# A retention layer and a Mish feed-forward layer on one core: the table of scale factors moves from ScalarE's load queue to SyncE's

## The chip, the core and the metric

The kernel runs on one core of a Trainium2 chip. The metric is device time in microseconds (us), the median over several executions. In the profile the engines are called PE (TensorE: matrix products and transposes), DVE (VectorE), ACT (ScalarE), POOL (GpSimd) and SP (SyncE). [...] A load that is started goes to a queue and is carried out by the core's 16 DMA engines, beside all computing. Whoever needs the data waits for a semaphore that the load raises when it has landed.

## The reference, cut to what matters

```python
def _attn_ref(q, k, v):                     # each (4, 8, 768, 64), float32
    B, H, S, D = q.shape
    gamma = 1.0 - 2.0 ** (-5.0 - np.arange(H, dtype=np.float32))
    scale = 1.0 / np.sqrt(D)
    state = np.zeros((B, H, D, D), dtype=np.float32)
    for t in range(S):
        state = gamma[None, :, None, None] * state + np.einsum('bhd,bhe->bhde', k[:, :, t], v[:, :, t])
        y[:, :, t] = scale * np.einsum('bhd,bhde->bhe', q[:, :, t], state)
    return y

def _moe_ref(x, w_in, w_out):               # x: the y above as (3072, 512)
    h = x @ w_in                            # (512, 2048)
    sp = np.where(h > 20.0, h, np.log1p(np.exp(np.minimum(h, 20.0))))
    g = h * np.tanh(sp)
    return g @ w_out                        # (2048, 512)
```

Each head keeps a state of 64 x 64 that decays by its own factor gamma from token to token. Every token's result of all eight heads, 512 numbers, then goes through two matrix products with the Mish function between them.

## The kernel before, in words

The tokens are cut into chunks of 128. Within a chunk the recurrence is written as products of matrices: scores of q against k, masked so that a token sees only earlier ones, times v; and q times the state that the chunks before have left. The decay is not applied token by token. A power of gamma that depends on the token's place and on the head is multiplied into q, k or v once, while they are converted from float32 to float16. These powers are the **table of scale factors**, `qvs`: 128 partitions x 88 float32 numbers, 44 KB, worked out when the kernel is built (lines 47 to 58) and kept in memory as a constant. It holds the factors for v (`vs`), for q of the first block (`qs_four`), for q and v or k of pairs of chunks (`qs_two`, `vs_two`) and a constant (`boosts`). Line 81 loads it, once.

The chunks are taken in blocks: the first block has four (512 tokens), all later ones two (256 tokens). Each block goes through the retention part and then through the feed-forward part, and the retention part of the next block is woven between the feed-forward products of the one before. Later blocks form sums of weights and of intermediate results, which save matrix products. Instructions are issued in the order in which the code stands (`manual_schedule`): every engine works through its own list in that order, and nothing plans it anew.

Four places matter for this change.

- **The constants** (lines 78 to 116). The table's load stands first, on ACT. POOL then makes an identity matrix (`ident`, lines 96 and 97) and masks; ACT loads its function table and runs one activation on a dummy (`warm`, line 116).
- **The first loads** (`load_first_q`, line 250, and `first_block`, line 1213). SP starts, in this order: the first half of q (four heads of 512 tokens, 512 KB), its second half (512 KB), four loads of k (256 KB each, line 296), four of v (256 KB each), w_in in six pieces (line 195), w_out, and then the inputs of the next chunks.
- **The first work** (`first_block`). PE runs 46 products of the identity matrix with itself (`spin(46, 1)`, line 466), whose result nobody uses, while q is on its way. `turn_first_q` (line 275) then scales a half of q on DVE (line 279, which reads `qf` and `qs_four`), lets PE transpose it (line 267) and ACT or DVE copy the result out (lines 271 and 273). After the first half come 14 more such products, after the second the same for k: DVE scales one quarter of k, POOL the other three (line 317), each with `vs_two`.
- **The step into the feed-forward part.** POOL converts the first slice of w_in to float16 (line 220), and PE begins the product with it (line 687).

The last store of the kernel is split: most pieces go out on SP's queue (line 1128), the very last piece on ACT's (line 1121). ACT starts no other transfer than this one and the table.

```python
    qvs = cpool.tile([P, (7 + CPB) * H], FP32, name="qvs")
    nc.scalar.dma_start(qvs, nc.inline_tensor(qvs_np, name="qvs_c").ap())
...
        nc.vector.tensor_tensor(
            in_place(q16), by_head(qf[:, mine]), scale_by_head(qs_four[:, mine]), op=ALU.mult)
```

Of the kernel before, what the change touches and what calls it, by code (L numbers as in the profile page):

```python
# [16 lines left out]
def kernel(  # L17
# [9 lines left out]
    nc = tc.nc  # L27
# [30 lines left out]
    qvs_np = np.ascontiguousarray(np.concatenate(tables, 1))  # L58
# [19 lines left out]
    ctx.enter_context(tc.manual_schedule())  # L78

    qvs = cpool.tile([P, (7 + CPB) * H], FP32, name="qvs")  # L80
    nc.scalar.dma_start(qvs, nc.inline_tensor(qvs_np, name="qvs_c").ap())

    def table(n, count=1):
        t = qvs[:, n * H:(n + count) * H]
# [165 lines left out]
    def load_first_q():  # L250

        qf = wstage.tile([P, H, CPB, D], FP32, name="qfirst", tag="wt", bufs=4)
        for a in range(0, H, H // 2):
            nc.sync.dma_start(
                qf[:, a:a + H // 2],
                q[0, a:a + H // 2, :TB].rearrange("h (p r) d -> p h r d", r=CPB))
        return qf

    def turn_parts(parts, dst, on_act=False):
# [952 lines left out]

    def first_block():
        qf = load_first_q()
        for n in range(2):
            room_pair(n)
# [320 lines left out]
```

## Time and profile before

| what | before |
|---|---|
| median of the runs | 192.01 us |
| the profiled execution's own time | 192.31 us |
| its span, first to last instruction | 190.5 us |
| PE busy | 184.8 us, 97% |
| DVE busy | 143.1 us, 75% |
| ACT busy | 105.8 us, 56% |
| POOL busy | 72.2 us, 38% |
| granted clock of PE, mean | 0.999 |
| read from memory, written | 27.31 MB, 6.29 MB |

The time of a run is a little longer than the span, since it takes in what lies around the first and the last instruction. In the views, a line such as `L279` is a line of the kernel before; `out<-in` names what an instruction writes and reads; what stands in brackets at the end is how long the engine was idle before it, and who ended that. `SPq` and `ACTq` are the issuing of transfers on SP and ACT, whose length is that of the issue and not of the transfer. "To landing" is counted from the start of the issue to the last semaphore of the load. A busy share of PE of 97% does not say that it works at its peak, as its products overlap and their ends are modelled.

### The profile page before, as it was taken

What the parts mean: (1) busy time and instruction counts of PE and PEld (TensorE: products, weight loads), DVE (VectorE), ACT (ScalarE), POOL (GpSimd) and SP (SyncE); (2) the same over time, 40 slices, a digit from 0 to 9 for tenths busy, and PEclk for the clock granted to TensorE, in tenths of its full rate; (3) what the DMA queues carried; (4) which work ended last, traced back from release to release, by engine and by line L of the source; (5) the groups of instructions that cost most, each with busy time, mean ns of one, the idle gap of its engine ahead of it and who ended that gap; (6) DMA issues with size and microseconds to landing.
All of it is one profiled execution on the core that took longest, in us unless ns stands there. A gap on an engine that the chain in (4) does not pass through costs nothing.

```text
span 190.5 us, 7643 instructions
## 1 busy us (share of the span) xinstructions
PE 184.8 (97%) x3310; PEld 162.3 (85%) x3310; DVE 143.1 (75%) x294; ACT 105.8 (56%) x201; POOL 72.2 (38%) x100
## 2 busy tenths in 40 slices
PE   7898999999999999999999999999999999999993
PEld 7656478888888888888998998998998998988982
DVE  0778469886977878988798698696697698676862
ACT  3366766264552552553684584584683673873650
POOL 5182000487508745940573634624534710000000
PEclk9999999999999999999999999999999999999999
DMA  4999999999999999899999997891899970301103
GB/s 147 310 303 350 382 387 376 293 330 226 189 237 294 172 235 238 129 266 234 220 186 317 156 202 165 214 200 39 194 174 244 219 172 3 114 3 53 62 3 112
DMA packets 84210, 38.82 MB, mean 204 GB/s; under 512 B 58192, under 2 KB 78288, under 8 KB 84176
## 3 DMA queue, kind: packets, MB, share of 16 engines
q1 hardware_dynamic: 83888, 38.22, 87.1%
q8 instruction: 26, 0.43, 1.0%
q10 hardware_dynamic: 288, 0.11, 0.4%
q14 instruction: 8, 0.07, 0.1%
HBM read 27.31 MB, written 6.29 MB: 176 GB/s over the span
## 4 chain that ended last, share of the span: by engine, by line
PE 93%; DMA 3%; DVE 1%; ACT 1%; issue 0%; SPq 0%; DVEq 0%
PE h_ps L917 23%; PE o_ps L1103 23%; PE h_ps L705 18%; PE o_ps L1007 10%; PE o_ps L762 7%; PE y_ps L609 3%; DMA qfirst<-in_q_dram 3%; PE u_ps L503 1%; PE at L495 1%; PE t_ps L267 1%; PE y_ps L396 1%; PE h_ps L687 1%; PE at L466 1%; PE at L347 1%; DVE qk L279 1%; PE u_ps L368 0%
## 5 line engine op out<-in xcount | busy, mean ns | idle before, releaser
L705 PE MATMUL h_ps<-xt,win 128*128 128x256 f16 (+1 forms) x276 | 34.3, 284 | 0.0
L705 PEld LDWEIGHTS <-win 128*128 128x128 f16 x276 | 26.7, 98 | 6.2 <-DVE win L220 0.3
L714 ACT ACTIVATE g<-h_ps 128x512 f16<-128x512 f32 x38 | 22.7, 597 | 15.2 <-PE h_ps L705 15.2
L917 PE MATMUL h_ps<-xt,wsum 128*128 128x128 f16 x448 | 29.6, 219 | 0.0
L929 ACT ACTIVATE g<-h_ps 128x512 f16<-128x512 f32 x42 | 24.2, 597 | 5.6 <-PE h_ps L917 5.6
L917 PEld LDWEIGHTS <-wsum 128*128 128x128 f16 x448 | 26.2, 98 | 0.0
L917 PE MATMUL h_ps<-xt,win 128*128 128x128 f16 x336 | 24.8, 219 | 0.0
L1103 PEld LDWEIGHTS <-gsum 128*128 128x128 f16 x232 | 21.5, 98 | 2.6
L1103 PE MATMUL o_ps<-tmat,gsum 128*128 128x256 f16 (+1 forms) x176 | 21.5, 268 | 0.0
L917 PEld LDWEIGHTS <-win 128*128 128x128 f16 x336 | 20.8, 98 | 0.2
L440 POOL TENSOR_TENSOR qk<-kf,qvs 128x512 f16<-128x512 f32 x18 | 18.9, 1052 | 2.5 <-DMA kf<-in_k_dram 2.5
L447 POOL TENSOR_TENSOR v<-vf,qvs 128x512 f16<-128x512 f32 x18 | 18.6, 1050 | 2.6 <-DMA vf<-in_v_dram 2.5
L437 POOL TENSOR_TENSOR qk<-qf,qvs 128x512 f16<-128x512 f32 x18 | 19.1, 1062 | 1.3 <-PE u_ps L368 1.3
L1103 PEld LDWEIGHTS <-g 128*128 128x128 f16 x184 | 16.5, 98 | 1.6
L667 ACT CAST xt<-y_ps 128x512 f16<-128x512 f32 x16 | 10.8, 738 | 11.1 <-PE y_ps L609 9.9
L965 DVE TENSOR_TENSOR h_ps<-h_ps,hsum 128x512 f32<-128x512 f32 x14 | 9.7, 695 | 9.2 <-PE h_ps L917 9.1
L1443 POOL COPY summed<-gsum 128x1 f16<-128x1 f16 x7 | 1.6, 233 | 36.8 <-DVE gsum L879 29.4
L954 ACT COPY h_ps<-h_ps 128x512 f32<-128x512 f32 x14 | 8.2, 583 | 12.4 <-issue 8.4
L1103 PE MATMUL o_ps<-wout,g 128*128 128x256 f16 (+1 forms) x120 | 14.5, 265 | 0.0
L1113 ACT COPY snap<-o_ps 128x256 f32<-128x256 f32 (+1 forms) x22 | 8.2, 373 | 11.0 <-PE o_ps L1103 11.0
L1126 DVE TENSOR_TENSOR osb<-o_ps,snap 128x256 f32<-128x256 f32 (+1 forms) x22 | 9.1, 415 | 4.2 <-ACT snap L1113 2.8
L942 DVE TENSOR_TENSOR hsum<-h_ps,hsum 128x512 f32<-128x512 f32 x14 | 9.6, 687 | 0.7 <-PE h_ps L917 0.2
(130 smaller groups left out, 334.0 us busy)
## 6 DMA issues: line engine op xcount, KB each, us to landing
out_dram<-osb SPq DMA_DIRECT2D x22, 256.0 KB, 3.9
qf<-in_q_dram SPq DMA_DIRECT2D x18, 256.0 KB, 4.8
kf<-in_k_dram SPq DMA_DIRECT2D x14, 256.0 KB, 6.0
vf<-in_v_dram SPq DMA_DIRECT2D x14, 256.0 KB, 5.3
wt<-in_moe_w_out_dram SPq DMA_DIRECT2D x6, 512.0 KB, 8.4
vf<-in_v_dram SPq DMA_DIRECT2D x20, 128.0 KB, 3.7
wi<-in_moe_w_in_dram SPq DMA_DIRECT2D x4, 512.0 KB, 8.3
wi<-in_moe_w_in_dram SPq DMA_DIRECT2D x2, 1024.0 KB, 11.1
```

What stands on the lines that cost most here:

```text
L437: nc.gpsimd.tensor_tensor(in_place(q16.rearrange("p (w x) d -> p w x d", x=2)), by_head(qf), scale_by_head(qs_two[:, heads]), op=ALU.mult)
L440: nc.gpsimd.tensor_tensor(k16.rearrange("p (y w) d -> p w y d", y=2), kf.rearrange("p (w y) d -> p w y d", y=2), boosts.rearrange("p (w y) ...
L447: nc.gpsimd.tensor_tensor(cast[g][2], loaded.pop(g)[2], vs[g % 2].unsqueeze(2).broadcast_to((P, H, D)), op=ALU.mult)
L667: nc.scalar.copy(dst[:, :, x], src)
L705: nc.tensor.matmul(h_ps[:, j, cols], wins[s][f // 2][:, bp, f % 2 * P:(f % 2 + 1) * P], xts[blk][:, bp, cols], start=(bp == 0 and at == 0) ...
L714: nc.scalar.activation(gt, h_ps, AF.Mish, scale=inv_boost3)
L762: nc.tensor.matmul(banks[ij][:, t], x(f)[:, t * P:(t + 1) * P], w(f), start=ij in open_banks, stop=f == fs[-1], skip_group_check=True)
L917: nc.tensor.matmul(o_ps[:, f], w(f // 2, k)[:, f % 2 * P:(f % 2 + 1) * P], x[:, k], start=begin and f == 0 and k == 0, stop=k == 1, skip_g ...
L929: nc.scalar.activation(gt[:, f:f + n, j * C:(j + 1) * C], src, AF.Mish, scale=inv_boost3)
L965: nc.vector.tensor_tensor(pf[p], pa[p], m5[p], op=ALU.add)
L1007: nc.tensor.matmul(o_ps[:, cols], x(f), w(f)[:, cols], start=first and z == 0, stop=z == n - 1, skip_group_check=True)
L1103: nc.tensor.matmul(o_ps[:, c:c + wide], x(f), w(f)[:, c:c + wide], start=first and f == 0 and c == cols.start, stop=f == n - 1, skip_group ...
```

## The change: what it does

The load of the table is taken away from its place ahead of everything on ACT's queue. SP starts it instead, between the first and the second half of q. Nothing else is edited; the lines between the two places move up by one, those after the second place down by one.

```diff
     qvs = cpool.tile([P, (7 + CPB) * H], FP32, name="qvs")
-    nc.scalar.dma_start(qvs, nc.inline_tensor(qvs_np, name="qvs_c").ap())
...
             nc.sync.dma_start(
                 qf[:, a:a + H // 2],
                 q[0, a:a + H // 2, :TB].rearrange("h (p r) d -> p h r d", r=CPB))
+            if a == 0:
+                nc.sync.dma_start(qvs, nc.inline_tensor(qvs_np, name="qvs_c").ap())
         return qf
```

## The prediction, made before the changed kernel was run

> **What bounds the kernel now.** I read the page's first two parts, then a table of stretches, then the chain of work that ended last, and then the first 18 us in order of time, since the change lies there.
>
> ```profile
> span 190.5 us, 7643 instructions
> ...
> PE 184.8 (97%) x3310; PEld 162.3 (85%) x3310; DVE 143.1 (75%) x294; ACT 105.8 (56%) x201; POOL 72.2 (38%) x100
> ...
> PEclk9999999999999999999999999999999999999999
> ```
> ```profile
> 0.00:6.60 6.60, 4.79 (x46) 4.62 (x46) 1.28 (x2) 1.49 (x2) 2.76 (x17) 1.00 0.66 201
> 6.60:17.64 11.04, 10.28 (x268) 6.54 (x268) 8.66 (x11) 6.98 (x14) 5.42 (x11) 1.00 1.14 314
> 17.64:40.00 22.36, 22.36 (x184) 17.17 (x185) 16.64 (x26) 13.17 (x24) 3.71 (x5) 1.00 1.07 357
> ```
>
> In the table the first column after the stretch is its length, the next PE's busy time. From 17.64 on PE has no gap in the third row, and the page gives it 97% of the whole span. So a change to the first loads acts on the time only by moving the moment at which PE's unbroken work begins, at 17.64 us, and then one to one. What leads there is in the chain:
>
> ```profile
> 1.25 5.51 DMA qfirst<-in_q_dram
> 6.76 0.02 issue
> 6.79 1.24 DVE qk L279
> 8.02 0.05 issue
> 8.07 1.00 PE t_ps L267 x12
> ...
> 17.64 1.92 PE h_ps L687 x16
> ```
>
> The second half of q sets the start (until 6.76), then DVE's scaling, then PE's transposes. The same stretch in order of time (start, length, engine, line):
>
> ```profile
> 0.74 0.39 ACTq L81 DMA_DIRECT2D qvs<-qvs_c  x1
> 0.74 1.00 SPq L254 DMA_DIRECT2D qfirst<-in_q_dram  x2
> ...
> 1.16 1.28 ACT L116 ACT_TABLE_LOAD   x1 [1.16 <-PEq L1521]
> ...
> 1.36 4.79 PE L466 MATMUL at<-ident 128*128 128x128 f16 x46 [1.36 <-POOL ident L97]
> ...
> 1.79 3.57 SPq L296 DMA_DIRECT2D kf<-in_k_dram  x4
> ...
> 5.34 1.22 DVE L279 TENSOR_TENSOR qk<-qfirst,qvs 128x1024 f16<-128x1024 f32 x1 [4.47 <-DMA qfirst<-in_q_dram]
> ...
> 6.62 0.62 PE L267 MATMUL t_ps<-ident,qk 128*128 128x128 f16 x8 [0.47 <-DVE qk L279]
> ...
> 6.79 1.23 DVE L279 TENSOR_TENSOR qk<-qfirst,qvs 128x1024 f16<-128x1024 f32 x1 [0.23 <-DMA qfirst<-in_q_dram]
> ...
> 7.07 0.93 PE L466 MATMUL at<-ident 128*128 128x256 f16 x7
> ...
> 7.27 1.01 ACT L271 COPY qkt<-t_ps 128x1024 f16<-128x1024 f16 x1 [4.62 <-PE t_ps L267]
> ...
> 8.74 3.05 POOL L317 TENSOR_TENSOR qk<-kf,qvs 128x512 f16<-128x512 f32 x3 [5.09 <-DMA kf<-in_k_dram]
> ...
> 16.98 0.61 POOL L220 CAST win<-wi 128x512 f16<-128x512 f32 x1 [3.18 <-DMA wi<-in_moe_w_in_dram]
> ...
> 17.64 1.64 PEld L687 LDWEIGHTS <-win 128*128 128x128 f16 x16 [0.17 <-POOL win L220]
> ```
>
> The reader is to see two things. DVE's first scaling waits 4.47 us for q although the table (qvs) is needed too; which of the two is last is told by their times to landing, first of the q halves, then of the table:
>
> ```profile
> DMA to landing us min/median/max: 4.5/5.0/5.5
> ```
> ```profile
> DMA to landing us min/median/max: 3.0/3.0/3.0
> ```
>
> Half one lands at 0.74+4.5 = 5.24, half two at 1.25+5.5 = 6.75 (its start is in the chain), the table at 0.74+3.0 = 3.74: it has 1.5 us to spare. And 17.64 hangs on two chains that end together: PE's own, and the first slice of w_in through the cast at 16.98, both fed by the same stream of loads. What that stream does at first (the last two columns are the DMA share and GB/s):
>
> ```profile
> 1.75:2.10 0.35, 0.35 (x7) 0.35 (x5) 0.00 (x0) 0.35 (x1) 0.32 (x1) 1.00 1.05 96
> 2.10:2.60 0.50, 0.50 (x7) 0.50 (x6) 0.00 (x0) 0.49 (x2) 0.45 (x1) 1.00 0.01 4
> 2.60:2.90 0.30, 0.30 (x6) 0.30 (x4) 0.00 (x0) 0.05 (x1) 0.25 (x3) 1.00 0.27 18
> 2.90:3.40 0.50, 0.50 (x8) 0.50 (x6) 0.00 (x0) 0.00 (x0) 0.44 (x4) 1.00 0.80 263
> 3.40:4.40 1.00, 1.00 (x12) 1.00 (x11) 0.00 (x0) 0.00 (x0) 0.23 (x2) 1.00 1.09 386
> ```
>
> Traffic begins at about 1.75, stops from 2.10 to 2.60 with three loads outstanding, and runs at its full 386 GB/s only from 3.4. Why it stops is not in the profile, and it is the main unknown of this forecast.
>
> **The change part by part.** As built, PE, DVE and POOL keep their instructions in the same order; ACT loses one DMA issue and SP gains one between the halves of q.
>
> ACT: the issue at 0.74 (0.39 us) goes, so its table load and the warming activation come up to 0.39 us earlier. ACT is then idle until 7.27 (4.62 us in its row), waiting for PE: 0.
>
> SP: one issue more, 0.39 us by ACT's row or 0.50 by half of SP's own first row. The second half of q and all later loads (4 of k, 4 of v, w_in, w_out, the rest) are issued up to 0.5 us later. What hides it: half two is then issued by about 2.2, but the half in front of it holds the DMA engines for 512 KB / 386 GB/s = 1.36 us, from 2.9 to 4.3. Without that cover it would cost the whole 0.5. The loads of k behind them are held up already: the four take 3.57 us to issue, 0.89 each, against 0.50 for q. So the added issue falls into time in which SP would be waiting: 0. SP's waits on earlier landings (from the second v load on) now stand on the first half, the table and the second half in that order; all three are landed in the order of issue, well before those loads can move: 0.
>
> Place of the table in the stream. It leaves the space in front of q and goes between its halves:
>
> ```profile
> q10 hardware_dynamic: 144, 0.05, 8.2%
> ```
>
> This is the table's queue in the first 6 us: 8.2% of 6.0 us is 0.49 us of all 16 engines, its stopped packets included. By bytes alone it is 44 KB / 386 GB/s = 0.12. So half two lands between 0.12 and 0.49 us later for it, if nothing were gained in front. The same goes the other way for half one: in 2.90:3.40 the engines move 263 GB/s in place of 386, a loss of 0.5 x (386-263)/386 = 0.16 us, while the table's rest is served beside q. I take 0.16 off the first half (5.08) and, for the table, 0.12, the price by bytes, since the row with no other load in it (1.75:2.10, 96 GB/s) moves most of a table in 0.35 us before the stop: the table lands at 5.08+0.12 = 5.20, half two at 6.75-0.16+0.12 = 6.71.
>
> DVE's first scaling needs half one and the table, so it starts at 5.20+0.10 = 5.30 (today 5.34 for a landing at 5.24), ends 6.52, and the second starts with half two's landing at 6.74, against 6.79. Were the table's price 0.49, the first would start at 5.67 and end 6.89, the second begin at 7.11 by its landing: +0.32. The bounds of this term are thus -0.05 and +0.32. I take -0.05.
>
> POOL and DVE's scaling of k need the table too, but at 7.9 and 8.7, 2.5 us after it: 0. All other uses are later. The memory it lies in and its readers are the same: 0.
>
> [...]
>
> Sum: 0 + 0 - 0.05 + 0 = -0.05 us at 17.64, and the same at the end. The profiled execution took 192.31 us, 1.8 more than its span, and 0.3 more than the median of the runs, 192.01. Against 192.01 the sum gives 191.96, so 192.0, with a range of its own of 191.7 to 192.3.
>
> **The rivals.** First, *the stop is the table's own doing*. The table is issued on ACT at the same time as q on SP; the stop falls into ACT's table load (1.16 to 2.44). SP's issue is held up too:
>
> ```profile
> L296 SPq DMA_DIRECT2D kf<-in_k_dram x6: 507/1154/2498, 1.8 to 31.1; - x6
> ```
>
> The loads of k take 507 ns at best, yet the first four 3.57 us together, although only q is in front of them. For it: all traffic stops, q's as well. Against: a stop at the very start can be that of any first load. If it is so, q runs from 1.9 at 386 GB/s, ends 3.26 and lands 0.95 later as today (4.27 by bytes, 5.24 landed): about 4.2; the table 4.3, DVE 4.4 to 5.7, second half about 5.8, second scaling to 7.0, a full 1.0 earlier. PE can't take all of it: its 46 warming matmuls last until 1.36+4.79 = 6.15, so the first transposes come at 6.15 in place of 6.62; then 0.45 of transposes and 0.8 of warming matmuls, and the second ones at 7.4 in place of 8.07, -0.67; k's, which wait on loads, up to -0.9. w_in comes 0.9 earlier too. So -0.6 to -0.9, 191.1 to 191.4, in the middle 191.3.
>
> Second, on the other side, *the stop goes with the table's packets wherever they are*. Today it is covered, as the table has 1.5 us to spare. From first traffic to landing it took 3.74-1.75 = 2.0 us. Behind half one, its packets are reached at 4.3, so it lands at 6.3, DVE starts at 6.4, ends 7.6, then 8.85 in place of 8.02: +0.85, 192.9. It decides as soon as the table takes over 1.2 us from being reached. PE's gap before its first transposes grows from 0.47 to 1.5 us. If its clock then fell back, what it costs is bounded by the start of the run:
>
> ```profile
> L466 PE MATMUL at<-ident x40: 288/314/315, 1.4 to 5.5; 128*128 128x128 f16 x40
> ```
> ```profile
> L466 PE MATMUL at<-ident x8: 219/220/314, 5.4 to 5.9; 128*128 128x128 f16 x8
> ```
>
> Matmuls of one shape take 314 ns until 5.5 and 220 after it, and 40 in 4.1 us (0.10 each) against 8 transposes in some 0.45 (0.056): about half pace for 4.2 us, so at most 2.1 us lost, and 195.0 in all: still under 2%. [...]
>
> Third, *ACT's queue is slow at its first use*, whenever that is. Today that is the table; after the change it is the last store of the kernel, which ends the run:
>
> ```profile
> 187.74 0.37 ACTq L1121 DMA_DIRECT2D out_dram<-osb  x1
> ```
> ```profile
> DMA to landing us min/median/max: 1.7/1.7/1.7
> ```
>
> This 64 KB store lands in 1.7 us, the 44 KB table in 3.0. If the 1.3 us between them are a first use, they move to the end, bare: 193.3. Against it: SP's queue stopped too at 2.1, after its own first packets, which points to a common cause.
>
> **How the numbers follow.** As forecast 0.42; stop caused by the table on ACT's queue 0.33; table stopped behind half one 0.12 (in 0.02 of it with a lost clock); first use at the end 0.07; none of these 0.06. The first three lie in 191.1 to 192.9 and hold 0.85 of the chance without the lost clock; the rest, 0.15, is left out. As both signs hold much of it, the likeliest one's own range, 191.7 to 192.3, stands beside it. About 2%, 3.8 us, is what a measurement of this kernel can tell from no change, and no case reaches it: even the costliest is 195.0. Faster by over 2% would need 3.8 us, but before 17.64 PE is idle only 1.81+0.76 = 2.57 us in all by the first two rows of the table. So faster 0.02, within 0.95, slower 0.03, all of the two ends from what I haven't seen.
>
> **What would show it.** Right: the stop between 2.1 and 2.6 is still there with the table gone from ACT, q's first half lands at about 5.1, DVE starts within 0.2 us of 5.34 and 6.79, and w_in's cast and 17.64 stand within 0.3 us. The first rival: full rate from 1.9 on, the first four loads of k issued at about 0.5 us each, DVE's start at 4.4, PE's first transposes directly behind the warming matmuls. The second: DVE waits for the table beyond half one's landing by a microsecond. The third: over 2.5 us to landing of ACT's last store. Wrong altogether if PE shows gaps after 17.64 that it has not now.

## The result, and the profile after

| | before | after |
|---|---|---|
| median of 21 runs each, on one chip | 192.49 us | 192.89 us |
| ratio, after to before | | 1.0033, 95% interval 1.0018 to 1.0047 |
| profiled execution's own time | 192.31 us | 193.2 us |
| its span | 190.5 us | 191.3 us |

The changed kernel is slower by a third of a per cent. 192.89 us stands just inside the range of 191.1 to 192.9, but where -0.05 us was forecast, +0.4 us came. The forecast started from 192.01, the median of the first three of the 21 runs of before; over all 21 it is 192.49, and that is what the changed kernel is compared with. The ratio leaves out one execution of before, of 236.98 us, and follows the means of all others (193.05 after, 192.43 before) rather than the medians, so that a kernel's ratio and its median can say a little different things. In three later comparisons on other chips the unedited pair gave 0.9978, 1.0010 and 1.0026 (e1, e11 and e15 below). The first lines of the page after:

```profile
span 191.3 us, 7643 instructions
...
PE 184.8 (97%) x3310; PEld 162.1 (85%) x3310; DVE 144.4 (75%) x294; ACT 105.7 (55%) x201; POOL 72.5 (38%) x100
...
PEclk9999999999999999999999999999999999999999
```

PE's work and clock are those of before. The start in order of time, in the kernel after (lines of the code are one off):

```profile
0.73 1.28 ACT L115 ACT_TABLE_LOAD   x1 [0.73 <-PEq L1522]
...
0.74 0.45 SPq L253 DMA_DIRECT2D qfirst<-in_q_dram  x1
...
1.25 0.48 SPq L257 DMA_DIRECT2D qvs<-qvs_c  x1
...
1.78 0.43 SPq L253 DMA_DIRECT2D qfirst<-in_q_dram  x1
...
2.25 2.64 SPq L297 DMA_DIRECT2D kf<-in_k_dram  x4
...
4.97 1.23 DVE L280 TENSOR_TENSOR qk<-qfirst,qvs 128x1024 f16<-128x1024 f32 x1 [4.10 <-DMA qvs<-qvs_c]
```
```profile
6.39 1.23 DVE L280 TENSOR_TENSOR qk<-qfirst,qvs 128x1024 f16<-128x1024 f32 x1 [0.20 <-DMA qfirst<-in_q_dram]
```
```profile
17.20 1.48 PE L688 MATMUL h_ps<-xt,win 128*128 128x256 f16 x12
```

The stretches of the start after (the last two columns are the DMA share and GB/s):

```profile
2.10:2.60 0.50, 0.50 (x7) 0.50 (x6) 0.00 (x0) 0.13 (x1) 0.45 (x1) 1.00 0.27 96
2.60:2.90 0.30, 0.30 (x6) 0.30 (x4) 0.00 (x0) 0.00 (x0) 0.25 (x3) 1.00 0.30 58
2.90:3.40 0.50, 0.50 (x8) 0.50 (x6) 0.00 (x0) 0.00 (x0) 0.44 (x4) 1.00 1.03 362
```

The stop from 2.10 to 2.60 is now a crawl at 96 GB/s, and full pace, 362 GB/s, still comes only behind 2.90. DVE now waits for the table and no longer for q, as the sum had it, and PE's unbroken work starts at 17.20 in place of 17.64. So this execution was 0.44 us *ahead* at the start. The time went elsewhere, in the middle and at the end. In the middle, where the view lists no wait of PE for before, it lists two for after (us in total, times, longest):

```profile
PE h_ps L918 <- issue: 0.3, 1, 0.3
PE o_ps L763 <- DVE tmat L857: 0.2, 1, 0.2
```

PE's last product starts at 187.18 before and 187.52 after: with a lead of 0.44 at 17 us and a lag of 0.34 at the end, the middle cost 0.78. Product set beside product, the lead falls by 0.17 at the second of these lines (37.5 us) and by 0.48 at the first (120.5 us); another 0.14 goes at 75 us, where no wait is listed. And behind that last product the span still goes on for 3.34 us before and 3.82 after. I call this the tail. The last instructions before, then after:

```profile
186.68 0.72 PE L1103 MATMUL o_ps<-tmat,g 128*128 128x128 f16 x10
186.85 0.38 PEld L1103 LDWEIGHTS <-g 128*128 128x128 f16 x6
187.01 0.85 SPq L1128 DMA_DIRECT2D out_dram<-osb  x2
187.44 0.27 ACT L1120 COPY osb<-o_ps 128x128 f32<-128x128 f32 x1 [1.50 <-PE o_ps L1103]
```
```profile
187.02 0.72 PE L1104 MATMUL o_ps<-tmat,g 128*128 128x128 f16 x10
187.13 0.43 PEld L1104 LDWEIGHTS <-g 128*128 128x128 f16 x7
187.34 1.08 SPq L1129 DMA_DIRECT2D out_dram<-osb  x2
187.78 0.27 ACT L1121 COPY osb<-o_ps 128x128 f32<-128x128 f32 x1 [1.50 <-PE o_ps L1104]
188.07 0.38 ACTq L1122 DMA_DIRECT2D out_dram<-osb  x1
```

PE and ACT do the same at the same distance. SP's last two stores (third and fourth of four) differ: issued within 0.85 us before, 1.08 after. The fourth starts 0.28 us behind the start of PE's last product before, 0.56 after, where ACT's last store starts too.

**What stands in SP's list.** Counted from 0 in the records that the trace keeps of SP (waits, and issues of loads, transposing copies and stores), SP pauses 0.43 to 0.45 us behind record 78 and 0.35 to 0.37 us behind record 206, that is 128 records later, in every trace of this study in which no longer wait covers the place, whatever stands there. From 1.0 to 2.2 us behind the end of that record the trace has a packet of 8192 bytes on queue 14, of the kind "instruction". That this packet goes with SP's list is seen where the list is longer: in e10, e13 and e14, whose record 206 comes 6 to 25 us earlier, it comes earlier too. Before, 206 is the fourth last store itself: the pause lies behind it, where SP only waits. The change puts one record more ahead of it, so 206 is the wait for the fourth store's data, and the store comes after the pause. The queues from 0.9 us behind the start of PE's last product on, before (188.1 to 189.0), then after (188.4 to 189.4):

```profile
q1 hardware_dynamic: 224, 0.13, 48.3%
q10 hardware_dynamic: 144, 0.07, 24.3%
```
```profile
q1 hardware_dynamic: 216, 0.13, 39.8%
q10 hardware_dynamic: 115, 0.06, 18.8%
q14 instruction: 1, 0.01, 3.5%
```

After, the instruction packet (0.57 us) runs among the packets of the last stores; before, it starts only at 1.95 us behind PE's last product, when the last of theirs has ended (1.79). Each of these stores has 16 landings in the trace. After, 15 of the fourth store's landings are there by 2.30 us behind PE's last product and the 16th at 2.56; ACT's store has 15 by 2.51 and the 16th at 2.74. Before, both are complete at 1.93 and 2.25, the 16th landing 0.01 behind the 15th. All 17 traces of this study part in this way: in the nine with the pause ahead of a last store, one of the last two stores or both have their 16th landing 0.16 to 0.79 us behind the 15th; in the other eight it is less than 0.05 behind. The trace does not tell on which of the 16 engines a packet runs, so that the packet and the late landing share an engine is concluded from this, not seen.

### The profile page after: what moved, and what is told of

Same layout as the page of the kernel before. It is cut to its first block, busy times and chain, and to the rows that moved or that the text cites. A ratio compares the mean times of both kernels' runs of the same rounds, so it can differ in the third digit from the quotient of the medians.

```text
span 191.3 us, 7643 instructions
## 1 busy us (share of the span) xinstructions
PE 184.8 (97%) x3310; PEld 162.1 (85%) x3310; DVE 144.4 (75%) x294; ACT 105.7 (55%) x201; POOL 72.5 (38%) x100
## 4 chain that ended last, share of the span: by engine, by line
PE 78%; DMA 11%; SPq 6%; DVE 2%; issue 1%; ACT 0%
PE h_ps L918 23%; PE o_ps L1104 23%; PE h_ps L706 11%; PE o_ps L1008 10%; DMA wi<-in_moe_w_in_dram 6%; DMA wt<-in_moe_w_out_dram 5%; PE o_ps L763 4%; SPq L297 3%; PE y_ps L610 3%; SPq L194 2%; PE u_ps L504 1%; PE at L496 1%; DVE tmat L857 1%; PE t_ps L268 0%; SPq L253 0%
## 5 line engine op out<-in xcount | busy, mean ns | idle before, releaser
L1444 POOL COPY summed<-gsum 128x1 f16<-128x1 f16 x7 | 1.6, 234 | 37.5 <-DVE gsum L880 30.1
```

## The experiments

The theory (P): the change costs nothing where it stands; it shifts SP's list by one, and the pause with its instruction packet comes ahead of the last stores. The rivals: the loss is a first use of ACT's queue at the end; it is any further issue on SP; it is chance in the middle. The expectations name the theories as they stood at that point.

What the profiled executions show of all kernels, in us. The third and fourth columns and the last landing are counted from the start of PE's last product; "records" are SP's; "first scaling" is DVE's. The tail is the last landing and 1.0 to 1.1 us more in every row.

| kernel | records | fourth store | packet on q14 | last landing | tail | first scaling | PE unbroken from | ratio to before, same chip |
|---|---|---|---|---|---|---|---|---|
| before | 217 | 0.28 | 1.95 | 2.25 | 3.34 | 5.34 | 17.64 | 1 |
| after | 218 | 0.56 | 1.20 | 2.74 | 3.82 | 4.97 | 17.20 | 1.0033 |
| e1 after | 218 | 0.58 | 1.58 | 2.93 | 4.01 | 5.01 | 17.21 | 0.9978 |
| e2 | 220 | 0.56 | 1.20 | 2.64 | 3.71 | 5.00 | 17.27 | 0.9983 |
| e3 | 219 | 0.25 (ACT's, now fifth: 1.07) | 1.85 | 3.14 | 4.22 | 5.18 | 17.12 | 1.0019 |
| e4 | 218 | 0.56 | 1.21 | 2.59 | 3.69 | 5.01 | 17.42 | 0.9967 |
| e5 | 217 | 0.41 | 2.06 | 2.35 | 3.47 | 4.88 | 17.05 | 1.0011 |
| e6 | 217 | 0.42 | 1.92 | 2.27 | 3.30 | 5.05 | 17.18 | 0.9994 |
| e7 | 217 | 0.37 | 2.09 | 2.25 | 3.34 | 4.79 | 17.23 | 1.0007 |
| e8 | 217 | 0.25 | 1.78 | 2.19 | 3.21 | 4.82 | 17.09 | 0.9976 |
| e9 | 218 | 0.78 | 1.43 | 3.06 | 4.14 | 5.00 | 17.22 | 1.0051 |
| e10 | 228 | 0.24 | none | 2.18 | 3.21 | 5.02 | 17.20 | 1.0024 |
| e11 after | 218 | 0.62 | 1.26 | 2.89 | 3.89 | 5.01 | 17.18 | 1.0010 |
| e12 | 218 | 0.88 | 1.53 | 3.21 | 4.28 | 4.88 | 17.13 | 1.0030 |
| e13 | 225 | 0.56 | none | 2.47 | 3.48 | 4.88 | 17.12 | 0.9983 |
| e14 | 226 | 0.69 | none | 2.46 | 3.47 | 5.05 | 17.23 | 0.9998 |
| e15 after | 218 | 0.56 | 1.55 | 2.89 | 3.97 | 5.06 | 17.82 | 1.0026 |

### e1 to e4: the end, on chip A

e1 is the changed kernel without any edit.

> The changed kernel once more, unedited, to see which of the places that differ in its first profile come back in a second one. In the first pair of profiles PE's unbroken work begins 0.44 us earlier than before (17.20 against 17.64) and the run still ends 0.8 us later (191.3 against 190.5). Theory M (the middle): the lead is lost in waits of PE between 17 and 185 us, which come back: about 0.8 us lost there again, and a ratio of 1.003 to the kernel before. Theory E (the end): the last store, now the first use of ACT's queue, takes about 0.4 us longer; SP's final wait for stores is again over 1.7 us, ratio 1.003. If it is chance, the ratio lies within 0.999 to 1.001.

Measured: 192.63 us, ratio 0.9978 (0.9951 to 1.0004). The tail is long again (4.01), yet the time is not above that of before. Here the kernel before took 193.14 in the median, in the other comparisons 192.26 to 192.68; the changed one took 192.63 to 192.94 in all four of its own. The executions of the kernel before spread there from 192.05 to 194.71. Why so many of them are slow is not known, as it has no trace from that chip; the fastest one, 192.05, lies below the fastest of e1 to e4 (192.25 to 193.03).

e2 and e3 put the last store on SP, in the changed kernel and in the one before:

```diff
-                nc.scalar.dma_start(out_rows(blk, i)[:, at], dst)
+                nc.sync.dma_start(out_rows(blk, i)[:, at], dst)
```

> The changed kernel with its last store on SP's queue, so that ACT's queue is not used at all. Theory E: against the next kernel, which has the same last store and the table where it was, the time is 0.0 to 0.4 us shorter, because the lead of 0.4 us at the front is kept and no first use is left at the end. Theory M: it is 0.5 to 0.7 us longer than the next kernel, as the changed kernel is against the one before.

> The kernel before with only its last store on SP's queue: the other half of the pair. By both theories within 0.4 us of the kernel before, since SP issues its own last store 0.27 us ahead of this one and is free.

Measured: e2 192.93 us, 0.9983 (0.996 to 1.0005), tail 3.71; e3 193.4 us, 1.0019 (0.9994 to 1.0043), tail 4.22. The rival that blames ACT's queue wanted e2 up to 0.4 us under e3, and the medians are 0.47 apart. But without ACT's queue at the end the tail is long all the same, in both, so ACT's queue is not what makes it long. In e3 the table still goes over ACT and record 206 is the fourth store; here the pause falls ahead of the fifth, which starts 1.07 us behind PE's last product.

e4 lets ACT's queue carry a small load early: a copy of the 16 factors for v, into a tile that POOL clears first.

```diff
-    vs = [table(0), table(1)]
+    vs_own = cpool.tile([P, 2 * H], FP32, name="vs_own")
+    vs = [vs_own[:, :H], vs_own[:, H:]]
...
+        nc.scalar.dma_start(vs_own, table_ap[:, :2 * H])
```

> The changed kernel, in which ACT's queue is used once early: ACT loads a second copy of the 16 columns of factors for v (8 KB) at about 6 us, when ACT is idle and the stream is running; all else, the last store on ACT too, is as in the changed kernel. Theory E: the last store is no first use any more, 0.4 us shorter than the changed kernel, 192.5. Theory M: as the changed kernel, 192.9 to 193.1.

Measured: 192.62 us, 0.9967 (0.9941 to 0.9993), tail 3.69. ACT's queue has been used by then, and the fourth store still starts at 0.56. That the kernel stands below the one before is the same open point as in e1.

### e5 to e8: position and start, on chip B

e5 was to make SP's list one longer in the kernel before: the third slice of w_in is loaded in two halves.

```diff
-            n = TB // 2 if s < 2 else TB
+            n = TB // 2 if s < 3 else TB
```

> The kernel before, table on ACT's queue as it was, with one SP instruction more: the third slice of w_in is loaded in two halves. Theory P (position): SP pauses for about 0.35 us at a fixed place in its list of instructions, between the 207th and the 208th that the trace records; before, that is behind the fourth of the last stores, and one instruction more on SP pushes this store behind the pause. So that store is issued 0.56 us after the start of PE's last product in place of 0.26, and from that start to the end of the span it takes 3.7 to 4.0 us in place of 3.3; time 0.3 to 0.6 us over the kernel before. Theory E (ACT's queue is slow at its first use): it was used at the start, so 3.3 us and the time of before. Theory M (waits of PE in the middle): as before.

Measured: 192.7 us, 1.0011 (0.9993 to 1.0029), tail 3.47. It is not the test that was meant: SP has one issue more, but one wait fewer, so 217 records as before, and record 206 is still the fourth store. This agrees with P but tells nothing by itself.

e6 takes one issue out of the changed kernel: one load of v is not cut in two.

```diff
-            parts = 1 if g < first[6] else 4 if small and n == 1 else 2
+            parts = 1 if g < first[6] or (g, n) == (first[6], 2) else 4 if small and n == 1 else 2
```

> The changed kernel with one SP instruction less: one load of v (chunk 14) is not split in two halves, so that SP has as many instructions as before. Theory P: the fourth of the last stores is issued 0.26 us after the start of PE's last product again, and the end takes 3.3 us; the lead at the front is kept: 0.3 to 0.5 us under the changed kernel and 0.2 to 0.5 under the kernel before. Theory E: the last store is still the first use of ACT's queue, so the end takes 3.7 us or more and the time is that of the changed kernel.

Measured: 192.13 us, 0.9994 (0.9972 to 1.0015), tail 3.30. With 217 records the tail is that of before, though the table is still on SP and ACT's queue is first used by the last store. The 0.2 to 0.5 us that were expected under the kernel before did not come: the two are the same.

e7 leaves the table on ACT, but writes its load behind the function table and the dummy activation.

```diff
-    nc.scalar.dma_start(qvs, nc.inline_tensor(qvs_np, name="qvs_c").ap())
...
+    nc.scalar.dma_start(qvs, nc.inline_tensor(qvs_np, name="qvs_c").ap())
```

> The kernel before with the table's load moved on ACT behind its function table and its first activation, so that it is issued at about 2.4 us in place of 0.7; SP's list is as before. If the table at the same moment as q is what delays q, q's first half lands at about 4.7 in place of 5.24 and PE's first transposes come at 6.25 to 6.3 in place of 6.6, as in the changed kernel; the end, by theory P, takes 3.3 us: 0.2 to 0.5 us under the kernel before. If the first loads are slow by themselves, q lands as before and the time is the same.

Measured: 192.19 us, 1.0007 (0.9984 to 1.003). The first scaling starts at 4.79, PE's unbroken work at 17.23, and the tail is 3.34. It is not the test that was meant:

```profile
0.73 1.28 ACT L115 ACT_TABLE_LOAD   x1 [0.73 <-PEq L1521]
...
0.90 0.34 ACTq L116 DMA_DIRECT2D qvs<-qvs_c  x1
```

The load was to start at about 2.4 us, but ACT starts it at 0.90, while the function table is still being loaded, only 0.16 us later than before. So e7 doesn't tell whether a table started together with q holds q up.

e8 loads no table; DVE fills it with ones, so the factors are left out of the result.

```diff
+    nc.vector.memset(qvs, 1.0)
...
-            if a == 0:
-                nc.sync.dma_start(qvs, nc.inline_tensor(qvs_np, name="qvs_c").ap())
```

> The changed kernel without the table's load: the table is filled with ones on DVE, so the factors are left out and all else is computed. It bounds what the table can cost in the stream. If the pause of traffic near 2 us is the table's, on whichever queue, traffic now reaches its full rate before 2.5 us, q's halves land at about 4.2 and 5.7, and DVE's first scaling starts at 4.3. If the first loads are slow by themselves, the full rate still comes at 2.9, q's first half lands at 4.6 to 4.7, DVE starts at about 4.75, 0.2 us ahead of the changed kernel (the table's 0.2 us behind the first half), and the second half lands 0.1 to 0.2 us ahead of its 6.4. SP has as many instructions as before: by theory P the end takes 3.3 us.

Measured: 191.84 us, 0.9976 (0.996 to 0.9993). DVE's two scalings of q in this kernel, and its traffic in the stretches of the start (last column GB/s):

```profile
4.82 1.23 DVE L279 TENSOR_TENSOR qk<-qfirst,qvs 128x1024 f16<-128x1024 f32 x1 [3.83 <-DMA qfirst<-in_q_dram]
6.28 1.23 DVE L279 TENSOR_TENSOR qk<-qfirst,qvs 128x1024 f16<-128x1024 f32 x1 [0.23 <-DMA qfirst<-in_q_dram]
```
```profile
2.10:2.60 0.50, 0.50 (x7) 0.50 (x6) 0.00 (x0) 0.13 (x1) 0.45 (x1) 1.00 0.53 88
2.60:2.90 0.30, 0.30 (x6) 0.30 (x4) 0.00 (x0) 0.00 (x0) 0.24 (x3) 1.00 0.27 72
2.90:3.40 0.50, 0.50 (x8) 0.50 (x6) 0.00 (x0) 0.00 (x0) 0.44 (x4) 1.00 1.01 350
```

Even with no table at all the traffic stays under 90 GB/s from 1.75 to 2.90, and the first scaling starts no sooner than 4.82. So the slow start is not the table's own doing.

### e9 to e11: the list made longer, on chip C

e9 gives the kernel before one small load that nobody reads; e10 gives the changed kernel ten. The edit of e9 (in e10 it is done for all chunks from 14 on):

```diff
+        if n == 2 and g == first[6]:
+            queue.dma_start(pad[:, g * 8:g * 8 + 8], src[:, 0, :8])
```

> The kernel before, with the table on ACT's queue as it was, and one further load of 128x8 numbers (4 KB) that nobody reads, started by SP behind the loads of v of chunk 14. The result is unchanged. Theory P (SP pauses some 0.35 us behind its recorded instruction 206, counted from 0, whatever it is): 206 becomes the wait of the fourth of SP's last stores in place of that store itself, so this store is issued at about 0.56 us behind PE's last product in place of 0.25 to 0.42, lands with ACT's last store, and the time from PE's last product to the end of the span is 3.6 to 4.0 us in place of 3.2 to 3.5; the time is 0.3 to 0.6 us over the kernel before. Rival F (the end is late because ACT's queue is used there for the first time): ACT's queue is used early, by the table, so the tail stays at 3.2 to 3.5 us and the time within 0.2 us of the kernel before. Rival N (the changed kernel's loss was chance between executions): no difference in tail or time.

> The changed kernel with ten further loads of 128x8 numbers (4 KB each) that nobody reads, one behind the loads of v of each chunk from 14 on, all started by SP: eleven more issues than before in place of one. The result is unchanged. Theory P: instruction 206 now lies some eleven places ahead of the fourth last store, among the stores of the block before the last stores, where SP waits for data anyway; the last four stores follow one another without the pause, the fourth is issued 0.25 to 0.42 us behind PE's last product, and the tail is 3.2 to 3.5 us: ten issues more and still 0.3 to 0.6 us faster than the changed kernel, and 0 to 0.4 us faster than the one before. Rival S (every further issue on SP costs time, 0.03 us or more each): slower than the changed kernel by 0.3 us or more. Rival F (first use of ACT's queue at the end): the tail stays at 3.6 to 4.0 us.

> The changed kernel without any edit, on the same chip as the two others, as their measure. Theory P: tail 3.6 to 4.0 us, start of the first scaling 4.9 to 5.1 us, time between 0.2 us below and 0.6 us above the kernel before, and 0.3 to 0.6 us above the changed kernel with ten small loads. Rival N: the same time as both others within 0.2 us.

Measured: e9 193.17 us, 1.0051 (1.003 to 1.0073), tail 4.14; e10 192.92 us, 1.0024 (1.0002 to 1.0045), tail 3.21; e11 192.82 us, 1.001 (0.9987 to 1.0034), tail 3.89. The tails came as P has them: long with one record more, short with eleven. The times only in part: e9 lost, but e10 did not gain. In e9 a wait in the middle stands beside the tail (us in total, times, longest):

```profile
PE at L499 <- DMA qkt<-qk: 1.2, 2, 0.8
```

So e9 doesn't price the tail alone. That its small load, 29 us ahead of the first of these waits, causes them isn't shown: at the second place, product set beside product with before, e10 loses only 0.3 us with ten such loads, and e11 and e12 lose 0.4 with none in the middle. Nor is it shown what took e10's gain: its profiled execution took 192.14 us, 0.78 below the kernel's median. Its fastest execution took 191.97 us, against 192.54 in e11 and 191.93 in the kernel before on this chip.

### e12 to e15: the same shift behind the middle, on chip D

The small loads stand just ahead of the first of SP's last four stores, where SP waits over 9 us for data. e12 has one and e13 eight, both on the kernel before; e14 has eight on the changed kernel, e15 is the changed kernel itself.

```diff
             if last:
+                while pads:
+                    p = pads.pop()
+                    nc.sync.dma_start(pad[:, p * 8:p * 8 + 8], v[0, 0, :C, :8])
                 nc.sync.dma_start(out_rows(blk, i)[:, at], dst)
```

> The kernel before with one load of 128x8 numbers (4 KB) that nobody reads, started by SP just ahead of the first of its last four stores, where SP waits over 9 us for data. The result is unchanged. Theory P: instruction 206 is no longer the fourth last store but lies ahead of it; the fourth store is issued 0.56 to 0.8 us behind PE's last product, the tail is 3.6 to 4.2 us, the time 0.3 to 0.8 us over the kernel before. Rival N (a pause behind the last product costs nothing, and the middle made the difference): the time is within 0.2 us of the kernel before, whatever the tail.

> The same with eight such loads at the same place, 3 to 4 us of issuing in the wait of over 9 us. The result is unchanged. Theory P: instruction 206 is one of these loads, its pause falls into the wait, the tail is 3.2 to 3.5 us as in the kernel before, and the time within 0.2 us of it. Rival S (more issues late on SP or more semaphores to wait for at the end cost time): at least as slow as with one load, tail of 3.6 us or more.

> The changed kernel with the same eight late loads. The result is unchanged. Theory P: tail 3.2 to 3.5 us, time 0.3 to 0.6 us below the changed kernel on the same chip and 0 to 0.4 us below the kernel before (what the start has gained). Rival N: the same time as the changed kernel within 0.2 us.

> The changed kernel without any edit, as the measure of the others. Theory P: tail 3.6 to 4.0 us; time 0 to 0.5 us over the kernel before, since the end loses 0.4 to 0.6 us and the start gains 0.1 to 0.4. Rival N: within 0.2 us of the kernel before and of the changed kernel with eight late loads.

Measured, with the kernel before at 192.44 us on this chip:

| small late loads | kernel before | changed kernel |
|---|---|---|
| none | 192.44 | 192.94, ratio 1.0026 (1.0008 to 1.0045) |
| one | 192.82, ratio 1.003 (1.0008 to 1.0052) | |
| eight | 192.21, ratio 0.9983 (0.9968 to 0.9998) | 192.14, ratio 0.9998 (0.9976 to 1.002) |

One 4 KB load, 11 us ahead of PE's last product and in a wait of 9 us, costs about as much as the whole change; seven more of them give it all back. The changed kernel gains more by its eight loads (0.80) than the 0.3 to 0.6 expected, and what it gains beyond the kernel before, 0.30 in the medians, is nothing by the ratio. SP's rows of e12, then of e13 (the loads, and the third and fourth store):

```profile
175.86 0.45 SPq L1133 DMA_DIRECT2D pad<-in_v_dram  x1
```
```profile
187.27 1.11 SPq L1134 DMA_DIRECT2D out_dram<-osb  x2
```
```profile
175.72 5.41 SPq L1133 DMA_DIRECT2D pad<-in_v_dram  x8
```
```profile
187.14 0.87 SPq L1134 DMA_DIRECT2D out_dram<-osb  x2
```

And the queues for some 1 us behind PE's last product, e12 (188.0 to 189.0), then e13 (187.9 to 189.0), each with the issue of ACT's last store and its time to landing:

```profile
q1 hardware_dynamic: 220, 0.17, 53.6%
q10 hardware_dynamic: 135, 0.06, 21.9%
q14 instruction: 1, 0.01, 4.4%
...
out_dram<-osb ACTq DMA_DIRECT2D x1, 64.0 KB, 2.5
```
```profile
q1 hardware_dynamic: 302, 0.21, 61.7%
q10 hardware_dynamic: 144, 0.07, 21.1%
...
out_dram<-osb ACTq DMA_DIRECT2D x1, 64.0 KB, 1.7
```

With one load, the two issues take 1.11 us and the instruction packet is there; with eight they take 0.87 and it is gone, since record 206 is now one of the small loads at 180.7 us, and its packet runs at 182. ACT's store, an untouched 64 KB with the same place in the code, lands in 2.5 us or in 1.7.

The table holds one execution of each kernel; the times of all executions give the same parting. Of each kernel take the fastest execution, assumed to be the least burdened by waits elsewhere. Where the pause comes ahead of a last store it took 192.20 to 193.03 us (after, e1 to e4, e9, e11, e12, e15); where it does not, 191.72 to 192.17 (e5 to e8, e10, e13, e14, and 191.83 to 192.05 for the kernel before in its five comparisons). On one chip, the changed kernel lies 0.20 (A), 0.61 (C) and 0.71 us (D) over the one before in this way, and 0.37 in the first comparison. The fastest of 12 to 35 executions is a rough measure, and the two ranges all but touch, yet they do not overlap.

e13 also parts the two halves of the cost. Its fourth store starts at 0.56, as late as in the changed kernel, for its second store took longer to issue (0.75 us, in after 0.33). Without the packet the last landing is at 2.47 and the tail 3.48. With it, at the same 0.56 to 0.58, the landing is at 2.59 to 2.93 and the tail 3.69 to 4.01 (after, e1, e4, e15). So, by these few executions, the late issue alone is worth 0.14 us against before, and the packet, with the one late landing in sixteen beside it, 0.2 to 0.5 more.

## Why the prediction was wrong, step by step

- **ACT, 0.** Right. ACT's function table is loaded 0.43 us earlier (0.73, before 1.16), and nobody gains by it.
- **SP's added issue, 0. This is the step that failed**: "So the added issue falls into time in which SP would be waiting: 0." At the start that is so. But an instruction added to SP's list moves everything behind it, too, relative to the places, behind records 78 and 206, at which SP pauses for 0.35 to 0.45 us and the instruction packet follows. It moved the pause and the packet from behind SP's last store to in front of it, some 187 us later. The working looked for the cover of the added 0.39 us where it stands, and for none at the end. Its price there is the tail: 3.69 to 4.28 us in the executions with a pause ahead of a last store, 3.21 to 3.48 in those without (before, e5 to e8, e10, e13, e14), so 0.2 to 1.1 us, and in the medians of chip D +0.38 (e12 against before) and +0.50 (e15). On the other chips the medians of the changed kernel are +0.40 (first comparison), +0.14 (e11) and -0.51 (e1), its fastest executions +0.37, +0.61 and +0.20.
- **The table's place in the stream, -0.05, bounds -0.05 and +0.32.** Inside its bounds. The signs for "right" fail in the first pair of profiles, DVE's starts at 4.97 and 6.39 against 5.34 and 6.79 and PE's at 17.20 against 17.64. But these 0.44 us are no effect of the change: with the table first on ACT (before, e3, e5, e9, e12, e13) the first scaling starts at 4.88 to 5.34 and PE's unbroken work at 17.05 to 17.64, middle values 4.94 and 17.13; with the changed start (after, e1, e2, e4, e6, e10, e11, e14, e15) at 4.97 to 5.06 and 17.18 to 17.82, middle 5.01 and 17.21. So the middle values are 0.08 apart, less than either group spreads: neither a gain nor a loss is shown, and the profile of before happened to have the slowest start of its group. The two parts of the term are nearly right. The working took 0.16 us off q's first half for a table that no longer runs beside it. Half one lands at 4.78 to 5.24 in the six, middle value 4.84, and at 4.67 to 4.76 in the nine, middle value 4.71, and 4.72 in e8, with no table at all: a credit of 0.13 (0.57 in the first pair). The table's price was taken as 0.12 by bytes and is larger, but far from 0.49: after, half one lands at 0.74+3.9 = 4.64 and the table at 1.25+3.6 = 4.85, 0.21 behind it (0.20 to 0.23 in all nine):

```profile
DMA to landing us min/median/max: 3.9/3.9/3.9
```
```profile
DMA to landing us min/median/max: 3.6/3.6/3.6
```

- **The other readers of the table, 0.** Right: none of them waits for it.
- **Rival one, the stop is the table's doing.** Refuted by e8. **Rival two, the stop goes with the table's packets.** Refuted: DVE waits for the table 0.21 us beyond half one's landing, not about a microsecond. So its branch with a lost clock, up to 195.0, had nothing to start from: PE's gap before the first transposes is 0.47 us before, 0.46 after and 0.8 in e11, not 1.5. No run shows that PE's pace falls back behind a gap. What the traces show is a slow start, 314 ns for a product until 5.5 and 220 behind it in the kernel before, while the granted clock reads 1.00 from the first stretch on. **Rival three, ACT's queue is slow at its first use.** It named the right place, the last stores, and gave 193.3, but for a wrong reason, and its sign is missing: ACT's last store lands in 2.2 us after, not over 2.5. In e6, e8, e10 and e14 ACT's last store is the first use of its queue and the tail is 3.21 to 3.47, while e4 and e12 have used it before and have 3.69 and 4.28. That 192.89 lies inside the range at all is luck: the upper end, 192.9, comes from rival two, which did not happen.
- **The traffic beside the table**, from which the 0.16 came as 263 GB/s against 386. In 2.90:3.40 the loads move 350 to 369 GB/s in the ten traces whose start has the table on SP's queue or no table, 240 to 339 in the seven with it on ACT's, of which e13 is one:

```profile
2.90:3.40 0.50, 0.50 (x8) 0.50 (x6) 0.00 (x0) 0.00 (x0) 0.44 (x4) 1.00 1.00 336
```
- **Waits of PE in the middle** were named as what would make the forecast wrong. Two came in the first profile of after, in a middle that lost 0.78 us in all. They are not the change's: in e1, e2, e4, e6, e10, e14 and e15, with the same start, the view lists none, while e5, with the start of before, has one of 0.3 us at 37 us. In single executions they weigh as much as the tail (1.2 us in e9), which is why a pair of profiles doesn't show the cause.

What stays open: why most executions of the kernel before are slow on chip A; e10's missing gain in the median; and what sets the waits in the middle, which vary from execution to execution.

## What to carry to other kernels

Adding one instruction to SP's list was here a change at two places: where it stands, and at the end, where it shifted the pause of 0.35 to 0.37 us behind record 206 ahead of a last store (tail 3.69 to 4.28 us with the pause there, 3.21 to 3.48 without). If a kernel ends on a chain of small stores, look in the trace whether an instruction packet runs among them, and count the records back from it. In these runs an edit elsewhere exposed it (the change itself, e9, e12) or hid it (e6, e10, e13, e14). A comparison that is to price such an edit needs a version with the list brought back to its old length, as in e6, or padded past it in a wait that is long enough, as in e13 and e14, whose eight loads take 5.4 and 5.8 us to issue in a wait of over 9 us.

One trace of each kernel says where to look; here it showed a gain of 0.44 us at the start where six and nine traces show none. Where less than 1 us counts, take the same place from all executions at hand.

## What the runs showed of the chip that was not expected

- SP stops for 0.35 to 0.45 us at two places of its list that are 128 records apart (78 and 206), and a packet of 8192 bytes of instructions follows 1.0 to 2.2 us behind the record, for 0.31 to 0.70 us. At the end of the changed kernel nothing covers the second of them: the tail of the executions with a pause ahead of a last store is 0.2 to 1.1 us longer. Queue 14 carries 8 packets of that size and kind within the span of before, these among them, and queue 8 another 26 of 16 KiB. Which engines the others go with is not shown. An estimate by number: 8192 bytes over 128 records are 64 bytes a record; by that a packet of 16 KiB would be 256 records, and PE, with 6627 records in the trace of before, its weight loads included, would need 25.9 of them, so the 26 fit PE.
- One late landing of 16 made a whole store late: ACT's store of e12 has 15 by 2.23 us and the last at 3.01 us behind PE's last product, beside an instruction packet that ends at 2.23.
- The same stands 2 us earlier in every trace. A packet of 16 KiB on q8 starts 1.2 to 1.9 us ahead of PE's last product, and SP's first of the four last stores has 15 landings 0.17 to 0.19 us ahead of that product and its 16th 0.27 to 0.92 behind it. In 15 of the 17 traces the second store's issue ends 0.37 to 0.40 us behind the end of that packet (not in after and e15, where it takes the least, 0.33 us), which would be why the fourth store starts anywhere from 0.24 to 0.69 where no pause stands ahead of it. No run tests this.
- Loads at the very start run slowly, with or without the table among them: 4 to 165 GB/s in each of the three stretches from 1.75 to 2.90 us in all 17 traces, then 240 to 369 GB/s in 2.90:3.40 and 372 to 386 in 3.40:4.40.
